# Two neighbouring rows of the second weight matrix to a partition, and every second column of the first as weights

## The chip, the core and the metric

The kernel runs on one core of a Trainium2 chip. The metric is the time of one execution in device microseconds (us). The engines are named as in the profile: PE is TensorE's matmuls, PEld its weight loads, DVE is VectorE, ACT ScalarE, POOL GpSimd, SP the engine that only issues DMAs.

## What is computed

Attention with 16 query heads and one shared key and value head, then a mixture of experts in two levels (4 groups of 4 experts). Each token goes to one expert; its two products are what the change is about.

```
scores = q @ k.T / sqrt(64)             # 8 batches, 16 heads, 384 tokens, 64 wide
attn   = softmax(scores) @ v            # x: 3072 tokens x 1024
g      = argmax(x @ w_group)            # 4 groups
e      = argmax(x[g] @ w_expert[g])     # 4 experts in the group
h      = maximum(x @ w1[g, e], 0)       # w1: 1024 x 1024 for each of 16 experts
out    = weight(g) * weight(e) * (h @ w2[g, e])
```

## The kernel before

The work is one long order written by hand: 96 slots of two attention units each (8 batches of 12 slots), with lists of steps that are hung on the slots by `at(slot, where, ...)`, and a generator of expert work that is moved on a few matmuls at a time by `advance`. Each engine runs its own instructions in this order.

For a batch, PE computes the scores (`scores`, line 206, f32, array tiles of 64 x 64), DVE takes the maximum (line 217), ACT the exponential (line 220), POOL divides (line 235), DVE transposes in blocks (line 241), and PE multiplies with v (`pv`, line 257, f32, array tiles of 32 x 64). The logits of the experts are line 280. Early units transpose q on PE (`q_group`, line 183, weights of 128 x 128 f32). `busy` (line 100) gives PE a few matmuls on zeros at the very start.

One expert, the one that most of the first 128 tokens of the batch chose, is run for the whole batch of 384 tokens, while the next batch's attention runs. `load_main` reads its number and calls `load_w` (line 451) for w1 and for w2: each matrix is loaded by two DMAs on POOL's queue (line 454), which turn f32 in memory into bf16 in SBUF. A tile `w` has 128 partitions, 8 chunks and 1024 columns. For w1 partition ki of chunk ko is row 128 ko + ki of the matrix, which is one input feature; for w2 partition fi of chunk fo is row 128 fo + fi, one hidden feature. There are two buffers for each matrix.

`expert` (line 472) does the two products. In the first, line 479, a block of 128 columns of w1 is the weights, and the 384 tokens of `xb` stream past; eight matmuls add up one block of 128 hidden features, which ACT or DVE moves to `h_t` with the maximum taken (lines 485 and 487). So partition i of `h_t[:, fc, :]` is hidden feature 128 fc + i. In the second, line 493, blocks of `h_t` are the weights, and 512 columns of w2 stream past. Both products of the last batch's expert (outputs named `sb` in the profile) run after the attention has ended.

In the last batch a second expert is loaded too (`load_second`) and run for at most 128 gathered tokens by `few_expert`: line 674 is its first product (64 matmuls of 128 columns), lines 680 and 682 the maximum, line 689 its second product (24 matmuls), lines 693 and 695 the scaling. Line 696 then writes its rows with an indirect DMA, the last step of the program. Pairs of batch and expert that are left over after that are run by a loop on the device; with these inputs it has nothing to do (the trace has 36 weight DMAs, for 8 + 1 experts).

The DMAs that load q, k and v and store the output stand on SP's queue; the weights stand on POOL's alone.

Of the kernel before, what the change touches and what calls it, by code (L numbers as in the profile page):

```python
# [12 lines left out]
P = 128  # L13
# [6 lines left out]
def kernel(  # L20
# [11 lines left out]
    nc = tc.nc  # L32
    B, H, S, D = q.shape
# [6 lines left out]
    KO = Dm // P  # L40
# [12 lines left out]
    QN = P // 32  # L53
    out_v = out.rearrange("(b j r n) d -> b j n r d", j=ST, n=QN, r=32)
    w1f = moe_w1.rearrange("g e (ko ki) f -> (g e) ki ko f", ki=P)
    w2f = moe_w2.rearrange("g e (fo fi) d -> (g e) fi fo d", fi=P)

    singles = ctx.enter_context(tc.tile_pool(name="singles", bufs=1))
    qpool = ctx.enter_context(tc.tile_pool(name="qpool", bufs=2))
# [33 lines left out]
    def xbank():  # L93
        x = ps_x.tile([P, 512], FP32, tag="x", name="x")
        return x
# [355 lines left out]
    def load_w(e, n):  # L451
        w = wpool.tile([P, KO, F], BF16, tag=f"w{n + 1}", name="w")
        for o in range(0, KO, 4):
            nc.gpsimd.dma_start(  # L454
                out=w[:, o:o + 4, :], in_=(w1f, w2f)[n][ds(e, 1), :, o:o + 4, :].rearrange("o p c f -> (o p) c f")
            )
        return w

    def load_main(b, n):
        if n == 0:  # L460
            st["e", b] = nc.gpsimd.value_load(st.pop(("idx", b))[0:1, 0:1], min_val=0, max_val=GE - 1)
        st.setdefault(("w", b), []).append(load_w(st["e", b], n))

    def load_second(n):
        if n == 0:
            st["e2"] = nc.gpsimd.value_load(st.pop("idx2")[0:1, 0:1], min_val=0, max_val=GE - 1)
        st.setdefault("w_second", []).append(load_w(st["e2"], n))
# [4 lines left out]
    def expert(xb, w1, w2, result, psum, on_act=None):  # L472

        on_act = on_act or (lambda k: k % 2 == 0)
        h_t = pool.tile([P, FO, S], BF16, tag="hT", bufs=1)
        for fc in range(FO):
            hp = psum()
            for ko in range(KO):
                nc.tensor.matmul(  # L479
                    out=hp[:, 0:S], lhsT=w1[:, ko, ts(fc, P)], rhs=xb[:, ko, :], start=(ko == 0), stop=(ko == KO - 1)  # L480
                )
                if ko % (KO // 2) == KO // 2 - 1:
                    yield
            if on_act(fc):
                nc.scalar.activation(out=h_t[:, fc, :], in_=hp[:, 0:S], func=ACTF.Relu)  # L485
            else:
                nc.vector.tensor_scalar(out=h_t[:, fc, :], in0=hp[:, 0:S], scalar1=0.0, scalar2=None, op0=ALU.max)
            yield
        for j in range(ST):
            for nh in range(2):  # L490
                yp = psum()
                for fo in range(FO):
                    nc.tensor.matmul(  # L493
                        out=yp, lhsT=h_t[:, fo, ts(j, P)], rhs=w2[:, fo, ts(nh, 512)],
                        start=(fo == 0), stop=(fo == FO - 1),
                    )
                    if fo % (FO // 2) == FO // 2 - 1:
                        yield
                result(j, nh, yp, on_act(FO + 2 * j + nh))
                yield  # L500
# [30 lines left out]
    def main_expert(b, on_act):  # L531
        w1, w2 = st.pop(("w", b))

        def store(j, y):
            for n in range(QN):
                nc.sync.dma_start(out=out_v[b, j, n], in_=y[32 * n:32 * (n + 1), :])

        yield from expert(st["xb", b], w1, w2, scaled(lambda: st["gsel", b][0], store), any_bank, on_act)
# [125 lines left out]
    def few_expert():  # L664

        fw = st["few"]
        w1, w2 = st.pop("w_second")
        xg, gate, at_ = fw["xg"], fw["gate32"], fw["at32"].bitcast(I32)
        h_t = pool.tile([P, FO, S], BF16, tag="hT", name="few_h", bufs=1)
        for k0, k1 in ((0, 4), (4, 6), (6, FO)):  # L670
            bank = xbank()[:, 0:(k1 - k0) * P]
            for k in range(k0, k1):
                for ko in range(KO):
                    nc.tensor.matmul(  # L674
                        out=bank[:, ts(k - k0, P)], lhsT=w1[:, ko, ts(k, P)], rhs=xg[:, ko, :],
                        start=(ko == 0), stop=(ko == KO - 1),
                    )
            h, hp = h_t[:, k0:k1, 0:P], bank.rearrange("p (k t) -> p k t", t=P)
            if k0 == 4:
                nc.vector.tensor_scalar(out=h, in0=hp, scalar1=0.0, scalar2=None, op0=ALU.max)  # L680
            else:
                nc.scalar.activation(out=h, in_=hp, func=ACTF.Relu)
        cols = ((0, 512), (512, 768), (768, Dm))
        ys = [xbank()[:, 0:z - a] for a, z in cols]
        y = pool.tile([P, Dm], FP32, tag="y", name="few_y", bufs=3)
        for part in range(2):
            for (a, z), yp in zip(cols, ys):
                for fo in range(4 * part, 4 * part + 4):
                    nc.tensor.matmul(  # L689
                        out=yp, lhsT=h_t[:, fo, 0:P], rhs=w2[:, fo, a:z], start=(fo == 0), stop=(fo == FO - 1)  # L690
                    )
                if part and a:
                    nc.scalar.activation(out=y[:, a:z], in_=yp, func=ACTF.Copy, scale=gate)
                elif part:
                    nc.vector.tensor_scalar(out=y[:, a:z], in0=yp, scalar1=gate, scalar2=None, op0=ALU.mult)
        nc.gpsimd.indirect_dma_start(
            out=out, out_offset=bass.IndirectOffsetOnAxis(ap=at_, axis=0), in_=y[:], in_offset=None,
            bounds_check=N - 1, oob_is_err=False,
        )
# [76 lines left out]
    for g in range(G):  # L776
        nc.sync.dma_start(
            out=wge[:, :, G + g * Eg:G + (g + 1) * Eg],
            in_=moe_w_expert[g].rearrange("(ko ki) e -> ki ko e", ki=P),
# [14 lines left out]
    for i in range(NSL):  # L794
        t, p = i // 4, i % 4
# [32 lines left out]
    i = NSL  # L828
# [25 lines left out]
    for n in range(4, 6):  # L854
# [14 lines left out]
        out=low, in_=low, pattern=[[-1, P]], compare_op=ALU.is_gt, fill=0.0, base=0, channel_multiplier=1  # L869
# [18 lines left out]
        out=sel[:], in0=iop, scalar1=pcum[:, 0:1], scalar2=pw[:, 0:1], op0=ALU.is_equal, op1=ALU.mult  # L888
# [17 lines left out]
    advance(1000)  # L906
    keep_xb(b)
    few_expert()

    n_rem = nc.values_load(lsi[0:1, NP:NP + 1], min_val=0, max_val=NP)  # L910
    with tc.For_i(0, n_rem, 1) as it:
        free.clear()
        e = nc.gpsimd.value_load(lse[0:1, ds(it, 1)], min_val=0, max_val=GE - 1)
        w1, w2 = load_w(e, 0), load_w(e, 1)
        bi = nc.sync.value_load(lsb[0:1, ds(it, 1)], min_val=0, max_val=B - 1)
        xr = pool.tile([P, KO, S], BF16, tag="xb", name="xr", bufs=2)
        nc.sync.dma_start(
            out=xr[:].rearrange("p c t -> p (c t)"), in_=xb_dram[ds(bi, 1)].rearrange("o p c -> (o p) c")
        )
        pid = nc.vector.value_load(lsi[0:1, ds(it, 1)], min_val=0, max_val=NP - 1)  # L920
        gcol = pool.tile([P, ST], FP32, tag="gcol")
        nc.vector.tensor_copy(out=gcol[:], in_=grem_all[:, ds(pid, 1), :].rearrange("p o j -> p (o j)"))
        bp = nc.gpsimd.value_load(lsb[0:1, ds(it, 1)], min_val=0, max_val=B - 1)

        def add(j, y):
            nc.gpsimd.dma_start(
                out=out_v[ds(bp, 1), j].rearrange("o n r d -> (o n) r d"), in_=y[:], accum_op=ALU.add
            )

        for _ in expert(xr, w1, w2, scaled(lambda: gcol, add), bank_end):  # L930
            pass
# [30 lines left out]
```

## Time and profile before

| what | us |
|---|---|
| runs of the kernel | 509.74, 509.68, 507.97 (median 509.68) |
| the profiled execution, whole | 508.39 |
| its span in the trace | 507.0 |
| PE busy in it | 481.5 (95%) |
| PEld busy | 262.1 (52%) |
| DVE busy | 413.0 (81%) |
| ACT busy | 321.8 (63%) |
| POOL busy | 289.6 (57%) |

The span goes from the first to the last instruction in the trace; the execution's own time has what lies around it too. Weight loads (PEld) run beside matmuls, so the two rows are not to be added. In the views, `128*128 128x384 bf16` is the part of the array that is used, then partitions x elements and the type. A row of the chain of waits is the start, the length, the engine, the tile that is written, the line and the number of instructions.

### The profile page before, as it was taken

What the parts mean: (1) busy time and instruction counts of PE and PEld (TensorE: products, weight loads), DVE (VectorE), ACT (ScalarE), POOL (GpSimd) and SP (SyncE); (2) the same over time, 40 slices, a digit from 0 to 9 for tenths busy, and PEclk for the clock granted to TensorE, in tenths of its full rate; (3) what the DMA queues carried; (4) which work ended last, traced back from release to release, by engine and by line L of the source; (5) the groups of instructions that cost most, each with busy time, mean ns of one, the idle gap of its engine ahead of it and who ended that gap; (6) DMA issues with size and microseconds to landing.
All of it is one profiled execution on the core that took longest, in us unless ns stands there. A gap on an engine that the chain in (4) does not pass through costs nothing.

```text
span 507.0 us, 20054 instructions
## 1 busy us (share of the span) xinstructions
PE 481.5 (95%) x8256; PEld 262.1 (52%) x8273; DVE 413.0 (81%) x737; ACT 321.8 (63%) x1002; POOL 289.6 (57%) x524
## 2 busy tenths in 40 slices
PE   7597789999999999999999999999999999999994
PEld 3143356555456455555465455555455455555653
DVE  3889979988899879988899879998799888890630
ACT  4776766677676766676676776676775775753421
POOL 1665955684576664584576654584476654584300
PEclk9999999999999999999999999999999999999998
DMA  7612997399947998389946998389956993089993
GB/s 106 145 26 45 174 239 193 76 160 233 255 86 129 220 237 218 75 157 232 261 84 123 217 243 223 75 143 230 245 116 111 210 241 110 1 155 241 231 243 121
DMA packets 64524, 84.04 MB, mean 166 GB/s; under 512 B 20379, under 2 KB 39963, under 8 KB 64432
## 3 DMA queue, kind: packets, MB, share of 16 engines
q0 software_dynamic: 19152, 37.84, 41.3%
q1 hardware_dynamic: 44320, 44.61, 35.2%
q8 instruction: 66, 1.08, 0.9%
q10 hardware_dynamic: 960, 0.30, 0.3%
q14 instruction: 26, 0.21, 0.1%
HBM read 101.52 MB, written 19.40 MB: 239 GB/s over the span
## 4 chain that ended last, share of the span: by engine, by line
PE 90%; DVE 5%; ACT 3%; issue 1%; POOL 0%; POOLq 0%; ACTq 0%; DVEq 0%
PE x L257 26%; PE s L206 25%; PE x L479 15%; PE x L493 13%; PE sb L493 4%; PE x L280 3%; ACT pr L220 3%; DVE nmx L217 2%; PE sb L479 2%; DVE ring L241 2%; PE x L674 1%; PE x L100 1%; PE x L689 1%; PE x L145 0%; PE x L643 0%
## 5 line engine op out<-in xcount | busy, mean ns | idle before, releaser
L235 POOL TENSOR_SCALAR pr<-pr,rinv 128x384 f32<-128x384 f32 x384 | 218.3, 588 | 146.0 <-DVE rinv L231 133.2
L220 ACT ACTIVATE pr<-s,nmx 128x384 f32<-128x384 f32 x384 | 218.0, 579 | 131.5 <-DVE nmx L217 120.0
L217 DVE TENSOR_REDUCE nmx<-s 128x2 f32<-128x768 f32 x192 | 174.3, 948 | 45.7 <-PE s L206 44.6
L241 DVE STREAM_TRANSPOSE ring<-pr 128x768 f32<-128x768 f32 x192 | 175.4, 952 | 0.1
L206 PE MATMUL s<-kt,qt 64*64 64x384 f32 x1536 | 148.9, 496 | 13.3 <-ACT pr L220 12.3
L257 PE MATMUL x<-ring,v_sb 32*64 32x256 f32 x4608 | 137.7, 378 | 0.2
L257 PEld LDWEIGHTS x<-ring,v_sb 32*64 32x64 f32 x4608 | 101.6, 131 | 43.0 <-issue 23.2
L206 PEld LDWEIGHTS s<-kt,qt 64*64 64x64 f32 x1536 | 48.5, 132 | 82.6 <-ACT pr L220 44.4
L220 ACT ACTIVATION_READ_ACCUMULATOR pr<-s,nmx 128x1 f32 x384 | 77.9, 203 | 0.0
L479 PE MATMUL x<-xb,w 128*128 128x384 bf16 x448 | 76.6, 326 | 0.0
L479 PEld LDWEIGHTS <-w 128*128 128x128 bf16 x512 | 47.7, 98 | 42.2 <-issue 12.6
L493 PE MATMUL x<-w,h_t 128*128 128x512 bf16 x276 | 64.7, 380 | 0.6
L493 PEld LDWEIGHTS <-h_t 128*128 128x128 bf16 x384 | 35.7, 98 | 52.0 <-issue 11.9
L454 POOL DMA_DIRECT2D w<-in_moe_w_dram x36 | 27.9, 784 | 10.8 <-issue 9.0
L271 ACT COPY xt<-x 128x256 f32<-128x256 f32 x96 | 28.9, 385 | 2.8 <-PE x L257 2.7
L485 ACT ACTIVATE h_t<-x 128x384 bf16<-128x384 f32 x56 | 25.4, 502 | 6.4 <-PE x L479 6.4
L272 POOL CAST xb<-xt 128x1024 bf16<-128x1024 f32 x24 | 24.9, 1036 | 3.6 <-ACT xt L271 3.6
L511 ACT ACTIVATE y<-x,gsel 128x512 f32<-128x512 f32 x36 | 24.8, 693 | 3.1 <-PE x L493 3.1
L195 DVE STREAM_TRANSPOSE qt<-q_sb 128x512 f32<-128x512 f32 x38 | 26.1, 687 | 0.0
L493 PE MATMUL sb<-w,h_t 128*128 128x512 bf16 x92 | 21.2, 379 | 0.2
L231 DVE RECIPROCAL rinv<-ssum 128x4 f32<-128x4 f32 x96 | 13.9, 144 | 3.3 <-ACT pr L220 3.3
L511 ACT ACTIVATE y<-sb,gsel 128x512 f32<-128x512 f32 x9 | 6.2, 688 | 16.1 <-PE sb L493 16.1
(132 smaller groups left out, 165.6 us busy)
## 6 DMA issues: line engine op xcount, KB each, us to landing
w<-in_moe_w_dram POOLq DMA_DIRECT2D x36, 1024.0 KB, 19.6
q_sb<-in_q_dram SPq DMA_DIRECT2D x76, 224.0 KB, 6.0
out_dram<-y SPq DMA_DIRECT2D x96, 128.0 KB, 6.3
xb_scratch<-xb SPq DMA_DIRECT2D x8, 768.0 KB, 4.3
v_sb<-in_v_dram SPq DMA_DIRECT2D x32, 96.0 KB, 4.0
kk<-in_k_dram SPq DMA_DIRECT2D x28, 92.0 KB, 4.1
q_sb<-in_q_dram SPq DMA_DIRECT2D x16, 128.0 KB, 3.3
q_sb<-in_q_dram SPq DMA_DIRECT2D x5, 64.0 KB, 3.1
```

The source lines that it names most:

```text
L195: nc.vector.transpose(out=qt[:].rearrange("p (x d) -> p x d", d=32), in_=q_sb[:, :, 0:32])
L206: nc.tensor.matmul(out=s[m * D:(m + 1) * D, h, 0:S], lhsT=qt[r, ts(2 * cc + m, D)], rhs=kt[r, :], start=True, stop=True, tile_position=(h ...
L217: nc.vector.tensor_reduce(out=nmx[:], in_=s[:, :, 0:S], axis=AX.X, op=ALU.max, negate=True)
L220: nc.scalar.activation(out=pr[:, h, :], in_=s[:, h, 0:S], func=ACTF.Exp, bias=nmx[:, h:h + 1], scale=1.0, accum_out=ssum[:, k, h:h + 1],)
L235: nc.gpsimd.tensor_scalar(out=pr, in0=pr, scalar1=rinv[:, k, h:h + 1], scalar2=1.0, op0=ALU.mult, op1=ALU.mult)
L241: nc.vector.transpose(out=ring[:, (u // 4) % 3, u % 4].rearrange("p h s -> p (h s)"), in_=st.pop(("pr", u))[:].rearrange("p h s -> p (h s)"),)
L257: nc.tensor.matmul(out=o[i][h * D:(h + 1) * D, 0:2 * P].rearrange("d (g c q) -> d g c q", g=2, c=4), lhsT=v_sb[r, n, :], rhs=ring[r, a:z + ...
L271: nc.scalar.copy(out=xt[:, :, ts(i, 32)], in_=o[:, 0:2 * P].rearrange("p (c q) -> p c q", c=KO))
L454: nc.gpsimd.dma_start(out=w[:, o:o + 4, :], in_=(w1f, w2f)[n][ds(e, 1), :, o:o + 4, :].rearrange("o p c f -> (o p) c f"))
L479: nc.tensor.matmul(out=hp[:, 0:S], lhsT=w1[:, ko, ts(fc, P)], rhs=xb[:, ko, :], start=(ko == 0), stop=(ko == KO - 1))
L493: nc.tensor.matmul(out=yp, lhsT=h_t[:, fo, ts(j, P)], rhs=w2[:, fo, ts(nh, 512)], start=(fo == 0), stop=(fo == FO - 1),)
L511: nc.scalar.activation(out=y[:, ts(nh, 512)], in_=yp, func=ACTF.Copy, scale=g)
```

## The change

The second matrix is laid out otherwise in SBUF: partition fi of the pair of chunks a holds rows 256 a + 2 fi and 256 a + 2 fi + 1 of w2, which lie side by side in memory. A piece of a transfer is then 8 KB of f32 in memory and 4 KB of bf16 in SBUF, where it was half of that; the number of DMAs and their bytes are the same. For the second product to add up the right features, `h_t` has to be in the same order, and that is done where its features are made: the weights of the first product are no longer 128 columns in a row but every second column of a block of 256 (`hidden`), even ones for an even `fc` and odd ones for an odd `fc`. Both first products take them so, in `expert` and in `few_expert`. The load of w1 and the second products read as before.

```diff
-    w2f = moe_w2.rearrange("g e (fo fi) d -> (g e) fi fo d", fi=P)
+    w2f = moe_w2.rearrange("g e (a fi c) d -> (g e) fi a (c d)", fi=P, c=2)
+
+    def hidden(w1, ko, fc):
+        a, c = fc // 2, fc % 2
+        return w1[:, ko, ts(a, 2 * P)].rearrange("p (i c) -> p c i", c=2)[:, c, :]
...
     def load_w(e, n):
         w = wpool.tile([P, KO, F], BF16, tag=f"w{n + 1}", name="w")
         for o in range(0, KO, 4):
-            nc.gpsimd.dma_start(
-                out=w[:, o:o + 4, :], in_=(w1f, w2f)[n][ds(e, 1), :, o:o + 4, :].rearrange("o p c f -> (o p) c f")
-            )
+            if n:
+                out_, in_ = w[:, o:o + 4, :].rearrange("p (a c) d -> p a (c d)", c=2), w2f[ds(e, 1), :, o // 2:o // 2 + 2, :]
+            else:
+                out_, in_ = w[:, o:o + 4, :], w1f[ds(e, 1), :, o:o + 4, :]
+            nc.gpsimd.dma_start(out=out_, in_=in_.rearrange("o p c f -> (o p) c f"))
         return w
...
-                    out=hp[:, 0:S], lhsT=w1[:, ko, ts(fc, P)], rhs=xb[:, ko, :], start=(ko == 0), stop=(ko == KO - 1)
+                    out=hp[:, 0:S], lhsT=hidden(w1, ko, fc), rhs=xb[:, ko, :], start=(ko == 0), stop=(ko == KO - 1)
...
-                        out=bank[:, ts(k - k0, P)], lhsT=w1[:, ko, ts(k, P)], rhs=xg[:, ko, :],
+                        out=bank[:, ts(k - k0, P)], lhsT=hidden(w1, ko, k), rhs=xg[:, ko, :],
```

## The prediction

> **What bounds the kernel now.** I read the page's head and its slices first, then the table of stretches, then the chain of waits.
>
> ```profile
> span 507.0 us, 20054 instructions
> ...
> PE 481.5 (95%) x8256; PEld 262.1 (52%) x8273; DVE 413.0 (81%) x737; ACT 321.8 (63%) x1002; POOL 289.6 (57%) x524
> ...
> PE   7597789999999999999999999999999999999994
> ```
>
> TensorE (PE) is busy 95% of the span, and from the seventh slice to the last but one it stands at 9. The table of stretches says how full that is; its columns are the length, then the busy time of PE, PEld (weight loads), DVE, ACT and POOL:
>
> ```profile
> 50.00:76.00 26.00, 21.70 (x468) 11.82 (x468) 22.25 (x34) 17.95 (x59) 19.31 (x31) 1.00 1.00 201
> 76.00:133.40 57.40, 57.30 (x1012) 30.91 (x1011) 50.86 (x86) 38.97 (x123) 36.81 (x65) 1.00 0.81 174
> ...
> 465.00:492.70 27.70, 27.64 (x243) 16.01 (x244) 12.05 (x45) 10.50 (x22) 5.96 (x18) 1.00 1.12 238
> 492.70:507.00 14.30, 7.40 (x89) 5.92 (x88) 1.93 (x3) 1.84 (x4) 1.11 (x1) 0.90 0.43 141
> ```
>
> From 76 us to 492.7 us PE leaves about 0.1 us in each 57 us: nothing but PE decides there, and whatever PE loses there is lost in full. Behind it comes a tail; the chain of waits gives its order (start, length, what):
>
> ```profile
> 486.20 6.91 PE sb L493 x32
> 493.11 3.57 PE x L674 x64
> ...
> 496.95 2.35 PE x L689 x14
> ```
>
> So the last expert's 64 first-product matmuls (line 674) stand on the path that sets the end, behind the 32 of line 493. No weight transfer stands on it.
>
> **The change, part 1: the load of w2 (line 454).** Each of the 36 weight DMAs moves 1024 KB. 18 of them are for w2.
>
> ```profile
> L454 POOL DMA_DIRECT2D w<-in_moe_w_dram x36 | 27.9, 784 | 10.8 <-issue 9.0
> ```
>
> ```profile
> q0 software_dynamic: 19152, 37.84, 41.3%
> ```
>
> ```profile
> 50.50 3.24 POOL L454 DMA_DIRECT2D w<-in_moe_w_dram  x4 [1.48 <-issue]
> ...
> 468.49 1.55 POOL L454 DMA_DIRECT2D w<-in_moe_w_dram  x2 [1.83 <-PE sb L493]
> ```
>
> ```profile
> DMA to landing us min/median/max: 19.7/22.5/25.4
> ```
>
> Queue 0 moves 37.84 MB in 19152 packets, 2 KB each, as many as 36 DMAs of 128 partitions by 4 pieces give (18432) with a few over. For w2 the pieces halve in number and double in size. A whole matrix, two DMAs, keeps the 16 engines for 0.413 x 507 / 18 = 11.6 us on average. What can that bring? POOL spends 784 ns on an issue. Lower bound of the price: the issue keeps its time, nothing gained. Upper bound: it halves, 18 x 0.39 = 7 us less of POOL. But PE is full from 76 us on, so only the issues before that, the first four at 50.50 us, could move the end: two of them are for w2, 2 x 0.39 = 0.8 us at most, and the one wait of PE's matmuls that comes often is for ACT:
>
> ```profile
> PE s L206 <- ACT pr L220: 12.3, 19, 1.6
> ```
>
> I take 0. The bytes stay as they are.
>
> The landing times are the cover on the other side. They are those of the two w2 transfers of the last expert, issued from 468.49 us on. They need up to 25.4 us, so the later lands near 469.3 + 25.4 = 494.7 us, and line 689 reads them from about 496.5 us. The slack is about 1.8 us. A faster transfer gains nothing there; a slower one is hidden until that is gone. No wait and no queue position is added or moved: the same engine issues the same number of DMAs in the same order.
>
> **Part 2: every second column as weights (lines 479 and 674).** This touches 512 + 64 weight loads, and no matmul gets more columns. First the loads as they are, by shape (mean ns after the busy time):
>
> ```profile
> L206 PEld LDWEIGHTS s<-kt,qt 64*64 64x64 f32 x1536 | 48.5, 132 | 82.6 <-ACT pr L220 44.4 <-issue 25.9 <-ACT h_t L485 5.6
> L479 PEld LDWEIGHTS <-w 128*128 128x128 bf16 x512 | 47.7, 98 | 42.2 <-issue 12.6
> ...
> L280 PEld LDWEIGHTS x<-xt,wge 128*32 128x32 f32 x1024 | 12.7, 110 | 5.5 <-ACT y L511 2.5 <-ACT pr L220 2.2 <-issue 0.8
> L183 PEld LDWEIGHTS x<-ident,q_sb 128*128 128x128 f32 x40 | 4.3, 142 | 6.3 <-issue 3.2 <-ACT xt L271 2.6 <-PE s L206 0.6
> L674 PEld LDWEIGHTS <-w 128*128 128x128 bf16 x64 | 3.7, 98 | 0.2
> ```
>
> How much of the 98 ns must lie in line one behind another? The first microseconds tell, where the array runs slower. Loads and matmuls of line 100, 128x512 (the first row is min/median/max of the loads, the others the timeline):
>
> ```profile
> L100 PEld LDWEIGHTS <-blank x6: 103/134/151, 1.7 to 5.5; 128*128 128x128 bf16 x6
> ```
>
> ```profile
> 2.08 0.15 PEld L100 LDWEIGHTS <-blank 128*128 128x128 bf16 x1 [0.28 <-issue]
> 2.50 0.15 PEld L100 LDWEIGHTS <-blank 128*128 128x128 bf16 x1 [0.28 <-issue]
> ```
>
> There a 512-column matmul comes every 0.42 us; in the tail 32 of them take 6.91 us, 0.216 us each. So the array is at half speed at the start. The load is 151 ns there and 98 ns later, a difference of 53 ns, and 128 columns at the full pace (512 in 0.213) are also 53 ns: the load is one column per array cycle, 53 ns, and 45 ns of fixed delay that overlaps with its neighbours. Now what the matmuls leave for it:
>
> ```profile
> 90.11 2.71 PE x L479 x16
> ...
> 133.41 4.01 PE x L479 x24
> ...
> 476.08 5.20 PE sb L479 x32
> ```
>
> ```profile
> 469.22 1.41 PE sb L479 x8
> ...
> 471.52 1.30 PE sb L479 x8
> ```
>
> ```profile
> PEld L479 <- issue: 12.6, 21, 0.6
> ```
>
> In line 479 a matmul takes 5.20 / 32 = 0.1625 us: a load may grow from 53 to 162 ns and stay hidden. In line 674 it takes 3.57 / 64 = 0.0558 us: there are 3 ns to spare, and all the rest shows, 64 times. Third, the groups of line 479 have a first load that nothing covers: 2.71 - 16 x 0.1625 = 0.11 us, 4.01 - 24 x 0.1625 = 0.11 us, and 0.11 us in the group at 469.22, but nothing in those that follow another bf16 group (1.30 = 8 x 0.1625). The waits count 21 groups that start behind the score matmuls, with the one at 469.22 there are 22.
>
> What does a load with a step of two bf16 elements cost? No row here shows one. Its addresses go in steps of 4 bytes, as those of f32 weights do, so the f32 rows are the nearest, though f32 may be slow for other reasons. Without the 45 ns: 128 columns of line 183 (142 ns) 97 ns; line 280 to line 206, 32 columns more for 22 ns, so 88 ns for 128; line 206 by itself, 64 columns in 87 ns, so 174 ns for 128. Below stands the load that notices nothing, 53 ns; a strided load has no reason to be faster. I take 97 ns, because line 183 has the same number of columns, partitions and the same step.
>
> The sum: line 674, 64 x (97 - 55.8) = 2.6 us; the 22 uncovered heads, 22 x (97 - 53) = 1.0 us; the other loads of line 479 nothing, the cover being a matmul of 162.5 ns. Together +3.6 us. The ends: 53 ns gives 0; 174 ns gives 64 x 118 + 22 x 121 ns + (512 - 22) x 11.5 ns = 7.6 + 2.7 + 5.6 = +15.9 us.
>
> [...]
>
> **How that stands to the runs.** The profiled execution took 508.39 us, 1.4 more than its span; the three runs have a median of 509.68 and go from 507.97 to 509.74. I use the middle of all four, 509.0. A measurement of this kernel can tell about 0.5% (2.5 us) from no change. Forecast: 509.0 + 3.6 = 512.6 us.
>
> **The rivals.**
>
> *The stride is free (not slower).* The load keeps its column per cycle, 53 ns, which is below 55.8 in line 674. Nothing is left but the gain of part 1, 0 to 0.8 us: 508.2 to 509.0. It decides as soon as the load stays below 84 ns: then 64 x 28 + 22 x 31 ns = 2.5 us. For it: no row shows that an address step costs anything by itself, and f32 rows carry twice the bytes. Against it: all f32 rows take more per column than 0.42 ns. [...]
>
> *The load outgrows its cover.* Above 162.5 ns all of line 479 pays, as the upper end shows: +15.9 us at 174 ns, 525 us. At four times 53 ns it would be 64 x 157 + 22 x 160 + 490 x 51 ns = 10 + 3.5 + 25 = +38.5 us, 547.5 us. For it only line 206 by itself; against it line 183 and the slope.
>
> *The second weight transfers become late.* If pieces of the new size run slower, the end of the queue slips. The last two w2 matrices would lose it twice: with 20% on 11.6 us each, 4.6 - 1.8 of slack = +2.8 us, 511.8 us. Against it: the bytes are the same, and fewer pieces have no reason to be slower. If the pieces are cut up again on the way, the load doesn't do what it says and part 1 is exactly 0.
>
> *Faster by 0.5%.* It would need 2.5 us of the 26.0 - 21.7 = 4.3 us that PE is idle between the first weight issue and the stretch that PE fills, and part 1 has 0.8 us at most to give there; behind 492.7 us no weight transfer is left to wait for.
>
> **How the numbers follow.** Forecast (load between 84 and 162 ns) 0.46, with its own range of 511.5 (+2.5) to 516.0 (162 ns: 64 x 106 ns + 22 x 109 ns = +9 us as its far end, most of it below +7); free stride 0.43, 508.2 to 511.5; outgrown cover 0.04; late transfers 0.03; faster 0.04. Slower 0.46 + 0.04 + 0.03 = 0.53, same 0.43, faster 0.04. The range takes the first two cases and the late transfers, without the thin upper end: 508.2 to 516.0.
>
> **What would show it.** The weight loads of lines 479 and 674 show their new duration: about 142 ns if I am right, 98 if the stride is free, above 207 if the cover is outgrown. The 64 matmuls of line 674 take 6.2 us in place of 3.57, groups of 32 in line 479 still 5.20, and a group of 16 some 2.75. POOL's issues for w2 show whether the pieces cost less. If line 689 waits for a DMA, the transfers were late. A load that stays at 98 ns, or a line 674 still at 3.57 us, makes the prediction wrong.

## The result, and the profile after

The changed kernel takes 511.19 us (median of 20 runs, 508.39 to 512.84), the kernel before 509.22 us (20 runs, 507.38 to 511.18). The ratio is 1.0036, with a 95% interval of 1.0024 to 1.0049: slower by about 1.9 us. The profiled execution took 509.69 us with a span of 508.2 us.

The loads that the change touches come first (groups by shape of the changed kernel; line 479 is now 486, line 674 is 681):

```profile
L486 PEld LDWEIGHTS <-w 128*128 128x128 bf16 x512 | 47.7, 98 | 42.2 <-issue 12.6
...
L681 PEld LDWEIGHTS <-w 128*128 128x128 bf16 x64 | 3.7, 98 | 0.2
```

98 ns with a step of two elements, as without it. The chain of waits at the end says the same of the matmuls, and something more:

```profile
475.46 5.20 PE sb L486 x32
...
492.49 3.57 PE x L681 x64
...
500.47 1.06 POOL out_dram L703
```

The last row in the kernel before was this:

```profile
501.08 1.05 POOL out_dram L696
```

The 32 matmuls still take 5.20 us and the 64 still 3.57 us. All of it comes 0.6 us *earlier* than before (line 674 started at 493.11, now at 492.49), and the last step of the kernel's own work, the indirect DMA, at 500.47 where it was 501.08. That much is the spread between executions: the unchanged kernel, profiled once more below (`e1_same_again`), came to its indirect DMA 0.85 us later than the first time. Yet the changed kernel's span ends 1.2 us later. So 1.8 us were lost behind the last line of the kernel that does any work. The chain ends with that DMA; what follows is its landing, 2.7 to 2.8 us after its start in both traces, and then sequencer instructions, which are not counted as busy and stand on no chain. They stand at the line that closes the program (957 before, 964 after). One kind of them is called DRAIN. Here are the DRAINs of POOL's queue: the count, the duration as min/median/max in ns, and the start of the first and of the last; first before, then after:

```profile
L957 POOLq DRAIN  x3: 46/103/1131, 505.0 to 506.7; - x3
```

```profile
L964 POOLq DRAIN  x3: 46/103/3091, 504.3 to 508.0; - x3
```

Three drains each, of which one is long: 1131 ns before, 3091 ns after, 1960 ns more. The long one comes first, at 505.0 us before and 504.3 us after, 1.2 us behind the landing of the last DMA in both, so it does not wait for that transfer. SP's queue goes on only when it is over; these are the instructions behind SP's wait, before and after:

```profile
L957 SPq EVENT_SEMAPHORE  x2: 17/17/17, 506.3 to 506.9; - x2
```

```profile
L964 SPq EVENT_SEMAPHORE  x2: 17/17/17, 507.6 to 508.2; - x2
```

505.0 + 1.13 is 506.1, and 504.3 + 3.09 is 507.4. The same shows in the waits of SP's queue near the end (total, times, longest; the profile puts them down to PE's queue, which waits at that place too), before and after:

```profile
SPq L957 <- PEq L957: 2.1, 2, 1.5
```

```profile
SPq L964 <- PEq L964: 4.0, 2, 3.5
```

The wait grows by the same 1.9 us (2.0 in the longest), and 1.96 us is 0.385% of 509 us, inside the interval of the ratio. The loads that the change was made for look as follows in the changed kernel:

```profile
L463 POOL DMA_DIRECT2D w<-in_moe_w_dram x36 | 27.1, 761 | 10.7 <-issue 6.6
```

```profile
q0 software_dynamic: 14544, 37.84, 39.6%
```

4608 packets fewer, 41.3% of the DMA engines' time down to 39.6%, and an issue of 761 ns on average in place of 784. None of it was on the path; the first four issues, the only ones before PE is full, took 3.18 us in place of 3.24.

### The profile page after: what moved, and what is told of

It is laid out like the page before. It is cut to its first block, busy times and chain, and to the rows that moved or that the text cites. A ratio compares the mean times of both kernels' runs of the same rounds, so it can differ in the third digit from the quotient of the medians.

```text
span 508.2 us, 20054 instructions
## 1 busy us (share of the span) xinstructions
PE 482.2 (95%) x8256; PEld 262.6 (52%) x8273; DVE 413.3 (81%) x737; ACT 321.4 (63%) x1002; POOL 287.7 (57%) x524
## 3 DMA queue, kind: packets, MB, share of 16 engines
q0 software_dynamic: 14544, 37.84, 39.6%
## 4 chain that ended last, share of the span: by engine, by line
PE 90%; DVE 4%; ACT 3%; issue 1%; POOL 0%; POOLq 0%; ACTq 0%; DVEq 0%
PE x L262 26%; PE s L211 25%; PE x L486 15%; PE x L500 12%; PE sb L500 4%; ACT pr L225 3%; DVE nmx L222 3%; PE x L285 2%; PE sb L486 2%; DVE ring L246 1%; PE x L681 1%; PE x L105 1%; PE x L696 1%; PE x L150 0%; PE x L650 0%
```

## The experiments

All ratios are against runs of the kernel before on the same chip, with 95% intervals. Since single executions of one kernel spread over some 4 us (507.38 to 511.18 in the 20 of the kernel before), the length of the long DRAIN, which the traces give to the nanosecond, is the sharper reading. The edits show the lines that matter, with comments added here.

**First: which part, and is it chance?** Theory A puts the time down to the pieces of w2 by way of the drain, theory B to the stride in executions that no profile showed, theory C to chance. Four kernels: the kernel before unchanged, each half of the change alone, and w1 in pairs of rows too.

> The kernel before, unchanged, as the measure of chance. Theory A (the new pieces of w2 lengthen POOL's drain at the end of the program): ratio 1.000 within 0.2%, POOL's long DRAIN at the end near 1.1 us as in the trace of before. Theory B (the strided weight loads cost time in executions that were not profiled): ratio 1.000 too, and nothing to be learnt from the drain. Theory C (the drain differs from one execution to the next by itself, the difference between the two traces is chance): the drain may well be 2 to 3 us here.

> Only w2 is loaded in pairs of rows; the first product takes its columns in a row as before, so the second product adds up features that do not belong together (the amount of work is the same). Theory A: ratio 1.0036, about +1.8 us, DRAIN near 3.1 us. Theory B: ratio 1.000. Theory C: ratio anywhere between, the drain no guide to it.

```diff
-  lhsT=hidden(w1, ko, fc)          # and in few_expert
+  lhsT=w1[:, ko, ts(fc, P)]
```

> Only the first products take every second column as weights; w2 is loaded as before, so the second product adds up features that do not belong together (the amount of work is the same). Theory A: ratio 1.000, weight loads 98 ns, DRAIN near 1.1 us. Theory B: ratio 1.0036, about +1.8 us. Theory C: no prediction beyond 1.000 plus or minus 0.4%.

```diff
-  if n:                            # w2 in pairs
+  if False:                        # w2 as before, from w2p = "g e (fo fi) d -> (g e) fi fo d"
```

> w1 and w2 are both loaded in pairs of rows, no stride in the weights, so both products add up features that do not belong together (the amount of work is the same). The suspected cost doubled. Theory A: DRAIN longer again, near 5 us, and the ratio near 1.007 (+3.6 us). Theory B: ratio 1.000. Theory C: as for the pieces of w2 alone.

```diff
+  w1q = moe_w1.rearrange("g e (a fi c) d -> (g e) fi a (c d)", fi=P, c=2)
-  if n:
+  if True:                         # both matrices in pairs, (w1q, w2f)[n]; contiguous weights as before
```

| kernel | ratio | interval |
|---|---|---|
| unchanged | 1.0002 | 0.9989 to 1.0015 |
| pieces only | 1.0025 | 1.0006 to 1.0044 |
| stride only | 1.0004 | 0.9990 to 1.0018 |
| both in pairs | 1.0037 | 1.0018 to 1.0055 |

The drains, in the same order (instructions of the closing line, POOL's queue):

```profile
L957 POOLq DRAIN  x3: 46/103/1131, 505.8 to 507.5; - x3
```

```profile
L964 POOLq DRAIN  x3: 46/103/3091, 505.7 to 509.3; - x3
```

```profile
L965 POOLq DRAIN  x3: 46/103/1131, 506.6 to 508.3; - x3
```

```profile
L965 POOLq DRAIN  x3: 46/103/3091, 504.7 to 508.3; - x3
```

The stride is free, and theory B falls: the stride-only kernel is not slower beyond its interval, and its loads of line 487 are 98 ns:

```profile
L487 PEld LDWEIGHTS <-w 128*128 128x128 bf16 x512 | 47.7, 98 | 42.2 <-issue 12.6
```

The drain is no chance, it repeats to the nanosecond, so theory C falls for it. It also accounts for the time: from the start of the indirect DMA to the end of the span lie 5.8 to 5.9 us in the three traces with the short drain and 7.7 to 7.9 us in the three with the long one. It goes with the pieces, as theory A said; but doubling the suspected cost did not double it. 3091 ns with half of the matrices in pairs and 3091 ns with all of them: not a price per piece. The issues and queue 0 with all of them in pairs:

```profile
L464 POOL DMA_DIRECT2D w<-in_moe_w_dram x36 | 26.6, 740 | 10.9 <-issue 6.8
```

```profile
q0 software_dynamic: 9936, 37.84, 38.1%
```

**Second: what of the pieces?** A large piece anywhere (A1), the pieces of the last DMAs (A2), or the number of pieces that the queue has carried (A3).

> Only the last two weight DMAs (w2 of the second expert in the last batch) have pieces of two rows, the other 34 are as before; no stride in the weights, so the last expert's product adds up features that do not belong together. About 18,900 packets on queue 0. Theory A1 (a large piece anywhere in the program lengthens the final DRAIN): 3.09 us, ratio near 1.003. Theory A2 (the pieces of the last DMAs decide): 3.09 us, ratio near 1.003. Theory A3 (not the size but the number of pieces that the queue has carried decides, and fewer of them make the DRAIN long): 1.13 us, ratio 1.000.

```diff
-  load_w(st["e2"], n)              # the second expert
+  load_w(st["e2"], n, True)        # True: w2 in pairs; all other calls False
```

> The eight main experts' w2 have pieces of two rows, the second expert's w2 in the last batch has single rows; no stride, so the main experts' products add up features that do not belong together. About 15,000 packets on queue 0. Theory A1: 3.09 us, ratio near 1.003. Theory A2: 1.13 us, ratio 1.000. Theory A3: 3.09 us, ratio near 1.003.

```diff
-  load_w(st["e", b], n)            # the main experts
+  load_w(st["e", b], n, True)      # the second expert: False
```

> All pieces are single rows, but only the first of the two DMAs of each w1 is issued, and the first products use that half twice; 27 weight DMAs, about 14,400 packets on queue 0, as few as in the changed kernel. The amount of work on TensorE is the same. Theories A1 and A2: 1.13 us, ratio 1.000 or a little less (less POOL work). Theory A3: 3.09 us, ratio near 1.003.

```diff
-  for o in range(0, KO, 4):
+  for o in range(0, KO if n else KO // 2, 4):
-  lhsT=w1[:, ko, ts(fc, P)]        # and in few_expert
+  lhsT=w1[:, ko % (KO // 2), ts(fc, P)]
```

> w2 in pieces of two rows as in the changed kernel, but w1 in pieces of half a row (two DMAs of 8 chunks by 512 columns), so that queue 0 carries about 23,800 packets, more than before; no stride, so the second product adds up features that do not belong together. Theories A1 and A2: 3.09 us, ratio near 1.003. Theory A3: 1.13 us or another length, the ratio follows it.

```diff
-  out_, in_ = w[:, o:o + 4, :], w1f[ds(e, 1), :, o:o + 4, :]
+  out_, in_ = w[:, :, ts(o // 4, 512)], w1f[ds(e, 1), :, :, ts(o // 4, 512)]
```

In that order, ratios of 0.9990 (0.9974 to 1.0007), 1.0021 (1.0002 to 1.0039), 1.0121 (1.0095 to 1.0146) and 1.0008 (0.9991 to 1.0024), and these drains:

```profile
L965 POOLq DRAIN  x3: 46/103/1131, 506.3 to 508.0; - x3
```

```profile
L965 POOLq DRAIN  x3: 46/103/3091, 506.0 to 509.7; - x3
```

```profile
L957 POOLq DRAIN  x3: 46/103/2356, 511.4 to 514.3; - x3
```

```profile
L964 POOLq DRAIN  x3: 46/103/1702, 507.3 to 509.6; - x3
```

The first has large pieces in its last DMAs and drains for 1131 ns, where A1 and A2 both said 3.09 us; the third has no large piece at all and still drains for 2356 ns. So A1 and A2 fall. A3 has the direction right (few pieces, long drain), but not the sizes. They are 1131, 1702, 2356 and 3091 ns: steps of 571, 654 and 735 ns, which are 7, 8 and 9 times 81.7 ns. And 9 is the difference in DMAs: the changed kernel has 36 weight DMAs (3091 ns), the one with half of w1 has 27 (2356 ns). From these two, 0.151 us and 0.0817 us for each DMA; by that 1131 ns are 12 DMAs and 1702 ns are 19, an estimate. That is theory D: the drain takes 0.151 us and 0.0817 us for each weight DMA that counts, all of those issued or, where it is short, fewer. The expectations below speak of entries that POOL clears off; that is the author's guess, and no trace shows an entry.

Half of w1 lost 6.0 us between the medians, of which the longer drain is 1.2. The other 5 or so lie in a part that the drain has no hand in. The chain of that kernel between two batches:

```profile
202.22 1.00 PE x L257 x18
203.22 0.56 issue
203.78 2.41 PE x L257 x78
```

PE stops for 0.56 us in the middle of a group, with nothing that the profile shows as the cause, and the group's 96 matmuls take 3.41 us besides, where the one before it takes 2.78. The like comes back at 261.63, 320.05 and 378.46 us (0.38 us the last time), once in a batch; the four together are about 4.6 us. What makes PE stop there was not tried.

**Third: the price per DMA, tried where it foretells a number.** One DMA per matrix and four, with the pieces unchanged.

> The changed kernel with one DMA for each matrix in place of two (18 weight DMAs, the same pieces). Theory D (POOL still has an entry for every weight DMA that it hasn't cleared off, and the final DRAIN takes 0.15 us and 0.082 us for each: 36 entries in the changed kernel, 27 with half of w1, 12 before): 18 entries, DRAIN near 1.62 us, so 1.5 us less than in the changed kernel and a ratio near 1.001. Theory A4 (the DRAIN follows the pieces on queue 0, below about 15,500 packets it is long): 3.09 us as in the changed kernel, ratio 1.002 to 1.004.

```diff
-  for o in range(0, KO, 4):        # and the slices, 4 -> 8 chunks
+  for o in range(0, KO, 8):
```

> The changed kernel with four DMAs for each matrix (72 weight DMAs, the same pieces). Theory D: if nothing is cleared off earlier, 72 entries, DRAIN near 6.0 us, +2.9 us over the changed kernel, ratio near 1.009; if a part is cleared off on the way, 0.15 us and a multiple of 0.082 us. Theory A4: 3.09 us, ratio 1.002 to 1.004.

```diff
-  for o in range(0, KO, 4):        # and the slices, 4 -> 2 chunks
+  for o in range(0, KO, 2):
```

> The kernel before with one DMA for each matrix (18 weight DMAs, single rows as pieces). Theory D: at most 18 entries, so at most 1.62 us; if POOL clears its entries at the same place in the stream of pieces as before, 6 entries are left, DRAIN near 0.64 us, ratio 0.999. Theory A4: 1.13 us as before, ratio 1.000.

```diff
-  for o in range(0, KO, 4):        # in the kernel before, and the slices
+  for o in range(0, KO, 8):
```

Ratios of 1.0010 (0.9994 to 1.0027), 1.0220 (1.0206 to 1.0234) and 1.0003 (0.9992 to 1.0015), and these drains:

```profile
L964 POOLq DRAIN  x3: 46/103/1627, 505.4 to 507.6; - x3
```

```profile
L964 POOLq DRAIN  x3: 46/103/6031, 512.1 to 518.7; - x3
```

```profile
L957 POOLq DRAIN  x3: 46/103/973, 506.4 to 507.9; - x3
```

1.62 was expected for 18 DMAs and 1.627 measured, 6.0 for 72 and 6.031 measured, with the same pieces in both: the price goes by DMAs, 0.0817 us each. With one DMA per matrix the changed kernel can't be told from the kernel before any more. The third number was missed: 0.973 us are 10 DMAs, not the 6 that I had expected to be left. With four DMAs per matrix the ratio was missed: near 1.009 was expected and 1.022 measured, so more is lost than the drain's 4.9 us over the kernel before. The first expert's first group started at 79.97 us in place of 76.19, and the issues cost more:

```profile
L463 POOL DMA_DIRECT2D w<-in_moe_w_dram x72 | 46.3, 665 | 11.0 <-issue 8.8
```

Of the 12.0 us by which this span is longer than that of the kernel before, 5.0 lie ahead of the last DMA and 2.2 between its landing and the drain. How much of the 5.0 hangs on these 46.3 us of POOL was not taken apart. To the 2.2 belongs an instruction called INC_SWDGE_SEM on POOL's queue, which comes behind the issue of the last DMA. It grows along with the drain; here it is before, in the changed kernel and with four DMAs per matrix, where it starts only when the DMA has landed (508.7 us) and is not hidden by the wait for it:

```profile
L911 POOLq INC_SWDGE_SEM  x1: 467/467/467, 501.7 to 501.7; - x1
```

```profile
L918 POOLq INC_SWDGE_SEM  x1: 947/947/947, 501.1 to 501.1; - x1
```

```profile
L918 POOLq INC_SWDGE_SEM  x1: 1647/1647/1647, 508.7 to 508.7; - x1
```

**Last: where the drain is shorter than the DMAs issued would make it.** By the fit above 36 DMAs are 3091 ns and 18 are 1621, but with 36 DMAs the loads of the kernel before, and those with pairs in the last expert alone, drained for 1131 ns, those in pairs and halves for 1702 ns, and with 18 the loads of the kernel before in one DMA for 973 ns. What these four ways of loading share is many packets on queue 0. A weight DMA has its pieces and 16 more there (before, 36 x (512 + 16) = 18432 + 576, and the 144 of the indirect DMA make the 19152); divided by the 16 engines that is pieces / 16 + 1. The kernels with 15120 packets (945 to an engine) or fewer drain for all their weight DMAs, those with 18640 (1165) or more for fewer. How many fewer is an estimate, worked out from the four drains by the price above and not counted in a trace: in that order 12, 12, 19 and 10 DMAs count. From these numbers and the packets the author fitted a rule, an estimate too: when the DMA that takes an engine past about 1,024 packets is issued, all but the latest 8 cease to count. It was tried on a kernel that passes that number twice:

> The kernel before with pieces of half a row for both matrices (36 weight DMAs of 8 chunks by 512 columns each, 128 rows of pieces per partition group, twice the pieces of before). A rule fitted to four runs is tried: counted for each of 16 engines, a weight DMA has its pieces / 16 + 1 entries in the stream (65 here, 33 before), and when the stream passes about 1,024, POOL clears off all but the last 8 DMAs. It gave 12 left before and with pairs in the last expert alone, 19 with pairs and halves, 10 with one DMA per matrix. Here the 16th DMA passes 1,024 and the 32nd passes 2,048. Rule with every 1,024: 12 left, DRAIN 1.13 us, ratio 1.000. Rule for the first pass alone: 28 left, 2.44 us, ratio 1.002. Nothing cleared off: 3.09 us, ratio 1.004.

```diff
-  out=w[:, o:o + 4, :], in_=(w1f, w2f)[n][ds(e, 1), :, o:o + 4, :]
+  out=w[:, :, ts(o // 4, 512)], in_=(w1f, w2f)[n][ds(e, 1), :, :, ts(o // 4, 512)]
```

```profile
L957 POOLq DRAIN  x3: 46/103/1131, 505.3 to 506.9; - x3
```

1.131 us, as the estimate with every 1,024 has it. Neither of its numbers is pinned down: the drains of all these kernels are fitted as well by 9 DMAs with any number from 1,057 to 1,072 packets as by 8 with 1,024 to 1,040. That anything happens on POOL at such a number was not shown.

The ratio went another way: 1.0028 (1.0014 to 1.0041) where 1.000 was expected. So about 1.4 us lie elsewhere. A part may be the clock: seven of the twelve executions were granted 0.992 of it or less, against four of seventeen of the kernel before, and if one compares those with each other and the rest with the rest, the medians differ by 1.0 and 0.9 us. The profiled execution was the fastest of twelve (508.67 us) and doesn't show where the time goes. Its issues are longer (916 ns against 784) and queue 0 takes more of the DMA engines:

```profile
L454 POOL DMA_DIRECT2D w<-in_moe_w_dram x36 | 32.6, 916 | 10.7 <-issue 8.9
```

```profile
q0 software_dynamic: 37584, 37.84, 46.2%
```

46.2% in place of 41.3%; that either is the cause was not shown.

## Why the prediction came out as it did

The forecast was slower by 3.6 us; measured were 1.9 us, from another place. The direction was right by luck: the one term that carried it measured 0, and a term put at nothing measured +1.96 us in its stead. The 511.19 us also lie just below the forecast's own case (511.5 to 516.0) and inside the range that the prediction gave to the free stride (508.2 to 511.5). By its own steps:

- *What bounds the kernel.* Right as far as it went: PE is full from 76 us to the tail, and the change left that stretch alone (57.30 of the 57.40 us from 76.00 on, before and after). But the reading stopped at the last instruction that is counted as busy. Between the indirect DMA at 501.08 us and the end of the span at 507.0 us lay 5.9 us, the landing of that DMA and then sequencer instructions alone, and the prediction had no term for that stretch.
- *Part 1, "I take 0".* This is the step that missed the cause, a term put at nothing. Both bounds were for the issue itself, 0 to 7 us of POOL hidden under PE. The measured gain in an issue was small: 784 to 740 ns when all 36 are in pairs, 44 ns each, not the 390 of the bound. The price of having fewer pieces came at the program's end, where nothing covers POOL: a drain of 3091 ns in place of 1131, 1960 ns more, by the estimate above 24 DMAs at 81.7 ns. "No wait and no queue position is added or moved" was true of the order written in the program and missed a wait that the program does not spell out, SP's at its closing line (longest 1.5 us before, 3.5 after).
- *Part 2, "I take 97 ns".* This is the step that gave the forecast, and it failed as well: a strided load stays at the 98 ns of one without a stride, 53 without the 45 that the prediction estimated as fixed, so its term is 0 in place of +3.6 us. (No row shows the prediction's 0.213 us for 512 columns; its rows give 6.91 / 32 = 0.216 us and so 54 ns for 128, beside the 53 of its other reading, 151 - 98; that changes nothing.) A step of 4 bytes alone does not slow a load (98 ns with it and without), so the nearest row, 128 columns of f32 at 142 ns, is slow for something else; the prediction named that doubt and then set it aside. What it is was not tried.
- *Its rivals.* The free stride was right about the loads (98 ns), and its time (508.2 to 509.0) was wrong for want of the drain. The outgrown cover and the late transfers did not happen: the second product, line 696 in the changed kernel, waits for no DMA in the chain. The signs that were to show the forecast (142 ns, 6.2 us) are absent, those against it (98 ns, 3.57 us) are there.

Still open: what POOL does in the 82 ns for a DMA, and why some kernels drained for less than their DMAs issued would make it. That the drain grows by DMAs was shown with counted ones (18, 27, 36 and 72 of them: 1627, 2356, 3091 and 6031 ns), and that fewer pieces of the same bytes lengthen it was shown too (3091 ns against 1131). Theory D foretold 1.62 us, it foretold 6.0 if every DMA issued counted, and 1.13 in one of the two forms of the fitted rule; it was wrong once (0.64 for 0.973), after which the rule was mended.

## What to carry to other kernels

The end of a program belongs to the path. Where a kernel issues DMAs from POOL, look at POOL's drain behind the last instruction, and count the weight DMAs rather than their bytes: here each cost 82 ns that nothing hides (drains of 2356, 3091 and 6031 ns for 27, 36 and 72 of them), and one DMA per matrix in place of two brought the changed kernel back to a ratio of 1.0010 (0.9994 to 1.0027). Before working on a transfer, ask whether anything waits for it; here the pieces became better and no one was waiting. And a price taken from the nearest row needs a reason why what makes that row slow is there in the new case too. Last, a total that lands in its range says little by itself: here two wrong terms made a right sum.

## What the runs showed of the hardware

- A weight load of 128 bf16 columns at every second element took 98 ns, as one of neighbouring columns does, also where 64 of them follow each other every 55.8 ns.
- POOL's long DRAIN at the program's end took 0.151 us and 0.0817 us for each weight DMA with 27, 36 and 72 of them, and within 6 ns of that with 18 (1627 ns). Where it was shorter than the DMAs issued would make it (973, 1131 and 1702 ns), how many count is an estimate worked out from it (10, 12 and 19). It was the same to the nanosecond in four kernels at 1131 and in four at 3091.
- The INC_SWDGE_SEM behind the issue of the indirect DMA grows along with the drain, from 467 to 947 and 1647 ns. In the changed kernel that was hidden, since POOL waited for the same DMA to land anyway (its longest wait there fell from 1191 to 657 ns).
- Pieces of 8 KB in memory used the DMA engines a little better than those of 4 KB: 38.1% of their time for the same 37.84 MB when both matrices had them, against 41.3%.
